# Attention with a gated MLP on one core: gating, last additions and row scaling moved from VectorE to GpSimd

## The chip, the cores and the metric

The kernel runs on one core of one Trainium2 chip. The metric is the time on the device in microseconds (us), the median of several runs. The time before is 1219.27 us, the median of 3 runs (1219.25 to 1219.4). The profile is of one execution of 1219.27 us, whose recorded span is 1217.5 us.

In the profile, PE is TensorE's matmuls, PEld its weight loads, DVE is VectorE, ACT is ScalarE, POOL is GpSimd, SP is SyncE. PSUM is the memory that matmuls write to, SBUF the on-chip memory that the other operands lie in.

## The reference

One input x (2048 rows of 512, bf16) is layer-normalised. The result feeds an attention with 32 heads against a cache of 2048 keys and values, and an MLP. The two are multiplied and added to x.

```python
xn = (x - mean) / sqrt(var + 1e-5)                 # per row of 512
q  = heads(xn @ wq)                                # 32 heads of 128
p  = softmax(q @ k_cache^T * 128 ** -0.5)          # 2048 x 2048 per head
s  = merge(p @ v_cache) @ wo                       # 2048 x 512
r  = max(xn @ w1 + b1, 0)                          # 2048 x 1792
g  = silu(r * r @ w2 + b2)                         # 2048 x 512
out = x + s * g
```

## The kernel before

The 2048 rows go in four blocks of 512 (j), each of four tiles of 128 rows (qt); jt is the tile's number, 0 to 15. Each block passes all 32 heads, each head in 8 steps of 256 keys (two tiles of 128), so that there are 1024 steps. At each step TensorE makes two score matmuls, ScalarE one exponential of 128x1024, and TensorE two matmuls with the values. All else (projections, MLP, output projection) is filled in between as single matmuls.

A small planner in the kernel's own source places every instruction on its engine's fixed list, from rough costs that it keeps of each. Three waiting lists matter here. `calm(due, fn)` puts a job on VectorE's list; `pool_quiet.append(fn)` puts one on GpSimd's list. The planner takes a job from them when it thinks that the engine is free and the job's inputs are there (`needs`).

The softmax's denominators need column sums of the exponentials pT. A pair is either reduced by VectorE alone (`den_part`), or GpSimd first adds its two halves into h_sum (`part_add`) and VectorE reduces that (`part_half`). The planner chooses by how much VectorE is behind. pT has 8 buffers, and an exponential waits until the one of 8 steps before has been read:

```python
def part_add(pi):                                   # GpSimd
    t_part[pi] = E(GP, partial(_tt, out=h_sum[:, x % NHS, :], in0=pT[:, pi % NPT, 0:QB],
                               in1=pT[:, pi % NPT, QB:2 * QB], op=ALU.add), ...)
    calm(pi + 6, partial(part_half, pi, x))          # then VectorE reduces h_sum
# ... in gen_scores:
    t_exp[pi] = E(AC, partial(_act, out=pT[:, pi % NPT, c0:c1], ..., func=ACT.Exp, ...),
                  deps=[t, t_PV[pi - NPT] ..., t_part.get(pi - NPT)])
```

The layer norm of the next block's rows (VectorE), transposed by DMA:

```python
def ln_scale(j, i):
    t_xn[jt] = E(DV, partial(_ts, out=ln_y(jt), in0=ln_x(jt),
                             scalar1=mv_t[:, i, 0:1], scalar2=rstd[:, i:i + 1],
                             op0=ALU.subtract, op1=ALU.mult), ...)
```

The gate. silu(z) = z/2 * (1 + tanh(z/2)), and the kernel keeps g_all = z * (1 + tanh(z/2)), twice the silu:

```python
# job_o2.evac: z from PSUM with the bias
tz = E(DV, partial(_tt, out=z_t[:, s, :], in0=bankF(bank), in1=b2bc[:], op=ALU.add), ...)
box[0] = E(AC, partial(_act, out=th_t[:, 0, :], in_=z_t[:, s, :], func=ACT.Tanh, scale=0.5), ...)
t_g[jt] = E(DV, partial(_stt, out=g_all[:, gs, :], in0=th_t[:, 0, :], scalar=1.0,
                        in1=z_t[:, s, :], op0=ALU.add, op1=ALU.mult), ...)
```

The output projection is summed in chunks of 8 heads into acc (float32, in SBUF). After the last but one chunk, acc is gated and x added; the last chunk is gated from PSUM and added to acc:

```python
if m == len(CH[j]) - 2:
    calm(step + 16, partial(acc_gate, j, qt))        # VectorE: acc = 0.5 * acc * g_all
    pool_quiet.append(partial(acc_add, j, qt))       # GpSimd:  acc = acc + x
if last:
    t = E(DV, partial(_stt, out=tmp_t[:, s, c0:c1], in0=place, scalar=0.5,
                      in1=g_all[:, jt % TPB, c0:c1], op0=ALU.mult, op1=ALU.mult), ...)
    eng = GP if j == NQB - 1 and qt in (0, 2) else DV
    t_fin[jt] = t_tmp[s] = E(eng, partial(_tt, out=row, in0=tmp_t[:, s, c0:c1],
                                          in1=acc[:, qt, c0:c1], op=ALU.add), ...)
    # ... and the DMA of the row to out
```

Of the kernel before, what the change touches and what calls it, by code (L numbers as in the profile page):

```python
# [5 lines left out]
ACT = mybir.ActivationFunctionType  # L6
# [53 lines left out]
def _cost(name, fn):  # L60
    f, k = fn.func, fn.keywords
    n = _elements(k["out"])
    if name == "PE":
        return n / 2.4 + 2.5, n / 2.4 + 166
    if name == "ACT":
        return n * 0.83 + 70, n * 0.83 + 172
    if name == "POOL":
        if f is _tt and n > 1:
            c = n * 2.3 + 55 if k["out"].tensor.name == "oT" else n * 2.05 + 60
            return c, c + 50  # L70
        return (500, 560) if f is _tt else (n + 100, n + 150)
    if f is _reduce_t:
        n = _elements(k["in_"])
    elif f is _reduce:
        n = _elements(k["in_"]) * 1.3 + 35
    elif f is _recip:
        n = n * 3.1
    elif f in (_bn_stats,):
        n = _elements(k["in_"])
    elif f is _ts and _in_sbuf(k["in0"]):  # L80
        n = n / 2
    return n / 0.96 + 70, n / 0.96 + 150


def _uses_port(name, fn):
    f, k = fn.func, fn.keywords
    if name == "POOL":
        return f in (_tt, _ts)
    if name == "DVE":
        if f in (_tt, _stt):  # L90
            return _in_sbuf(k["in0"]) and _in_sbuf(k["in1"])
        if f in (_ts, _copy):
            return _in_sbuf(k.get("in0", k.get("in_")))
    return False
# [206 lines left out]
def bass_recurrent_scan__mha_block_cached__dense_activation_squared_relu__prompt_kernel(  # L301
# [186 lines left out]
    def ln_y(jt):  # L488
        return out_t[:, jt - 2, :] if 2 <= jt < TPB else xn_t[:, jt % 2, :]
# [30 lines left out]
        ln_bn(j, i)  # L520
        ln_rstd(j, i)

    def ln_scale(j, i):
        jt = j * TPB + i
        assert jt < TPB or ln_prev(jt) in t_xnr
        t_xn[jt] = E(DV, partial(_ts, out=ln_y(jt), in0=ln_x(jt),
                                 scalar1=mv_t[:, i, 0:1], scalar2=rstd[:, i:i + 1],
                                 op0=ALU.subtract, op1=ALU.mult),
                     deps=[t_xr[jt], t_xnr.get(ln_prev(jt))])
# [7 lines left out]
        assert j < 2 or n_xuse[j - 2] == NFC + H  # L537

    def ln_next(j, i):
        ln_scale(j, i)  # L540
        ln_transpose(j, i)
        if i + 2 < TPB:
            ln_load(j, i + 2)
# [346 lines left out]
    def needs(fn):  # L890
        f, a = fn.func, fn.args
        if f in (den_part, part_half):
            m = b_no[a[0] // NPR]
            if m >= 2 and m - 2 not in t_sum:
                return None
            return [t_exp[a[0]]] if f is den_part else [t_part[a[0]]]
        if f in (den_sum, den_turn, den_write, den_read, den_total, den_recip, rec_write,
                 rec_read, den_scale):
            g = a[0]
            m = b_no[g]  # L900
            if f is den_sum and tiles[g] < NPR:
                return None
            first, before = {
                den_sum: (t_parts.get(g, []), t_row), den_turn: ([t_sum.get(m)], t_dw),
                den_write: ([t_row.get(m)], t_dr), den_read: ([t_dw.get(m)], t_tot),
                den_total: ([t_dr.get(m)], t_rw), den_recip: ([t_tot.get(m)], {}),
                rec_write: ([t_rec.get(m)], t_spr), rec_read: ([t_rw.get(m)], t_scale),
                den_scale: ([t_col.get(m), t_spr.get(m)], {})}[f]
            if m >= 2 and f not in (den_recip, den_scale):
                first = first + [before.get(m - 2)]  # L910
            return first
        if f is norm_recip:
            return t_oev[a[0]]
        if f is norm_scale:
            return [t_rden.get(a_no[a[0]])]
        if f is acc_gate:
            return [t_acc[a[1]], t_g.get(a[0] * TPB + a[1])]
        if f is acc_add:
            jt = a[0] * TPB + a[1]
            return [t_ug.get(jt), tok_xt.get(jt)]  # L920
        if f is ln_bn:
            return [t_xl.get(a[0] * TPB + a[1])]
        if f is ln_rstd:
            return [t_bn.get(a[0] * TPB + a[1])]
        if f is ln_next:
            return [t_xr.get(a[0] * TPB + a[1])]
        return gate_needs[fn]

    def ready_at(fn):
# [217 lines left out]
    def job_o2(j, qt):  # L1147
        jt = j * TPB + qt

        def mm(n, bank):  # L1150
            t = E(PE, partial(_mm, out=bankF(bank), lhsT=h2T[:, n, qt * P:(qt + 1) * P],
                              rhs=w2_sb[:, n, :], start=(n == 0), stop=(n == NFC - 1)),
                  deps=[tok_w2, t_bankF[bank], t_h2[j, n]], inc=(n == NFC - 1))
            if t is not None:
                assert n_w2[0] == NFC // 2
                t_o2[j, qt] = t
                t_o2j.append(jt)

        def evac(bank, step):
            s = jt % 2  # L1160
            assert jt < 1 or jt - 1 in t_g
            tz = E(DV, partial(_tt, out=z_t[:, s, :], in0=bankF(bank), in1=b2bc[:], op=ALU.add),
                   deps=[t_o2[j, qt], tok_b2, t_zrd[s], t_tmp[s]])
            box = [None]

            def gate():
                gs = jt % TPB
                t_g[jt] = t_zrd[s] = t_thr[0] = E(
                    DV, partial(_stt, out=g_all[:, gs, :], in0=th_t[:, 0, :], scalar=1.0,
                                in1=z_t[:, s, :], op0=ALU.add, op1=ALU.mult),  # L1170
                    deps=[box[0], t_fin.get(jt - TPB)])

            def tanh():
                box[0] = E(AC, partial(_act, out=th_t[:, 0, :], in_=z_t[:, s, :], func=ACT.Tanh,
                                       scale=0.5), deps=[tz, t_thr[0]])
                fn = partial(gate)
                gate_needs[fn] = [box[0]]
                calm(step + 8, fn)

            at(step + 1, tanh)  # L1180
            return tz
        return NFC, mm, evac

    t_fin = {}

    def job_wo(j, m, qt, c0=0, c1=D):
        jt = j * TPB + qt
# [15 lines left out]
        def evac(bank, step):  # L1203
# [2 lines left out]
                    t_wodone[j * H + h] = box[0]  # L1206
            place = (bankF(bank) if isinstance(bank, int) else bank[0])[:, 0:c1 - c0]
            if m == 0:
                t_acc[qt] = t = E(DV, partial(_copy, out=acc[:, qt, :], in_=place),
                                  deps=[box[0], t_fin.get(jt - TPB)])  # L1210
            elif not last:
# [1 line left out]
                                              in1=acc[:, qt, :], op=ALU.add),  # L1213
                                  deps=[box[0], t_acc[qt]])
            if m == len(CH[j]) - 2:
                calm(step + 16, partial(acc_gate, j, qt))
                pool_quiet.append(partial(acc_add, j, qt))
            if last:
                s = jt % 2
                assert all(x in t_g for x in t_o2j)  # L1220
                t = E(DV, partial(_stt, out=tmp_t[:, s, c0:c1], in0=place, scalar=0.5,
                                  in1=g_all[:, jt % TPB, c0:c1], op0=ALU.mult,
                                  op1=ALU.mult),
                      deps=[box[0], t_g[jt], t_tmp[s], t_zrd[s]])
                end = jt >= NQB * TPB - 2
                row = (x_t if end else out_t)[:, s, c0:c1]
                eng = GP if j == NQB - 1 and qt in (0, 2) else DV
                t_fin[jt] = t_tmp[s] = E(
                    eng, partial(_tt, out=row, in0=tmp_t[:, s, c0:c1],
                                 in1=acc[:, qt, c0:c1], op=ALU.add),  # L1230
                    deps=[t, t_u[jt], None if end else t_outdma[s]])
                eng, sl = (SP, sl_fin) if j == NQB - 1 else (GP, sl_out)
                dma = S.emit_dma(
                    eng, partial(_dma, out=out[0, jt * P:(jt + 1) * P, c0:c1],
                                 in_=row), sl[s], deps=[t_fin[jt]])
                if c1 == D:
                    t_outdma[s] = dma
            return t
        return nh, mm, evac

    def load_xt(jt):
        if jt < NQB * TPB:
# [3 lines left out]

    def acc_gate(j, qt):
        jt = j * TPB + qt
        t_ug[jt] = E(DV, partial(_stt, out=acc[:, qt, :], in0=acc[:, qt, :], scalar=0.5,
                                 in1=g_all[:, jt % TPB, :], op0=ALU.mult, op1=ALU.mult),  # L1250
                     deps=[t_acc[qt], t_g[jt]])


# [115 lines left out]
                                        in_=bass.AP(tensor=B_b2.tensor, offset=B_b2.offset,  # L1369
                                                    ap=[[0, P], [1, D]])), sl_b2)  # L1370

    at(62, load_b2)
    for i in range(2):
        at(140 + 8 * i, partial(load_xt, i))
    tok_w2 = None
# [14 lines left out]
    for j in range(NQB):  # L1390
        if j + 1 < NQB:
            for i in range(TPB):
# [2 lines left out]
                b = j * SPB + 8 * NPR + 4 * NPR * i  # L1395
                at(b, partial(calm, b + 32, partial(ln_bn, j + 1, i)))
                at(b, partial(calm, b + 32, partial(ln_rstd, j + 1, i)))
                at(b, partial(calm, b + 32, partial(ln_next, j + 1, i)))


    HD = D // 2
# [149 lines left out]
```

The softmax here doesn't subtract the row's maximum and nothing guards it: scores larger than these inputs give would overflow.

## Time and profile before

| | before |
|---|---|
| time, median of 3 | 1219.27 us |
| span of the profile | 1217.5 us |
| granted TensorE clock | 1.00 |
| matmul on TensorE | 1206.4 us, 6150 records |
| exponentials on ScalarE | 1036.6 us, 1025 |
| h_sum additions on GpSimd | 863.0 us, 758 |
| reductions of h_sum and of pT on VectorE | 495.2 us, 758; 215.4 us, 178 |

The busy row gives each engine's busy time and its share of the span. The chain of waits follows the last instruction back, at each step to what released it, and so names the work that set the end. A row of the groups names the operation, the tile written and the tiles read, their shapes, the count, the busy time, the mean of one in ns, and then the idle time in front of them with what ended it. In the profile's rows L239, L245, L249 and L253 are helpers through which many operations go, so the groups are told apart by their tiles. z_t is also the buffer of the last chunk's product (tmp_t is another name for it).

### The profile page before, as it was taken

The page shows a single profiled execution, that of the slowest core. Times are in us where ns is not written, and L with a number is a line of the kernel's source. Part 1 is how long each engine was busy: PE and PEld are TensorE (multiplying, and loading weights), DVE is VectorE, ACT ScalarE, POOL GpSimd, SP SyncE. Part 2 cuts the span into 40 slices and gives each one's busy share as a digit, 9 for nine tenths or more (in the row PEclk, how much of TensorE's full clock was granted, in tenths as well). Part 3 has the DMA queues.
Part 4 walks back from the last instruction along what each step waited for, and adds up shares of the span by engine and source line. Part 5 has one row for each costly group of instructions (what it writes and reads, how often), then busy time and mean ns, then how long its engine had stood idle before and what let it go on. Part 6 is the DMA issues. An engine that isn't in the chain of part 4 may idle for free.

```text
span 1217.5 us, 19712 instructions
## 1 busy us (share of the span) xinstructions
PE 1206.4 (99%) x6150; PEld 668.3 (55%) x6269; DVE 1067.2 (88%) x1865; ACT 1090.4 (90%) x1162; POOL 1064.2 (87%) x982
## 2 busy tenths in 40 slices
PE   9999999999999999999999999999999999999999
PEld 7555555555555555555555555555555555555556
DVE  4798889899999898879999999888999999889973
ACT  7898989999899898999989999999999999989995
POOL 1687999999898899999888899999998889999981
PEclk9999999999999999999999999999999999999999
DMA  9889888888778786777787777877778777677781
GB/s 209 182 202 211 193 181 168 187 170 184 179 157 178 170 161 155 164 159 153 169 167 159 171 167 166 163 163 164 163 163 167 164 164 164 158 160 164 160 156 49
DMA packets 510009, 203.47 MB, mean 167 GB/s; under 512 B 421808, under 2 KB 493744, under 8 KB 509904
## 3 DMA queue, kind: packets, MB, share of 16 engines
q1 hardware_dynamic: 507808, 198.13, 76.2%
q0 software_dynamic: 1424, 3.81, 1.1%
q8 instruction: 50, 0.82, 0.3%
q14 instruction: 55, 0.45, 0.1%
q10 hardware_dynamic: 672, 0.26, 0.1%
HBM read 128.23 MB, written 4.25 MB: 109 GB/s over the span
## 4 chain that ended last, share of the span: by engine, by line
PE 95%; DVE 3%; issue 1%; POOL 1%; ACT 0%; ACTq 0%; POOLq 0%
PE psA L226 36%; PE psO L226 32%; PE psF L226 24%; PE psO L231 3%; DVE d_part L286 1%; DVE acc L249 1%; POOL h_sum L239 0%; ACT pT L235 0%; PE psA L231 0%; DVE qt_sb L253 0%; DVE acc L239 0%; DVE d_sum L282 0%; PE psF L270 0%; POOL oT L239 0%; POOL acc L239 0%
## 5 line engine op out<-in xcount | busy, mean ns | idle before, releaser
L235 ACT ACTIVATE pT<-psA 128x1024 bf16<-128x1024 f32 x1025 | 1036.6, 1025 | 108.2 <-PE psA L226 71.2
L239 POOL TENSOR_TENSOR h_sum<-pT 128x512 f32<-128x512 bf16 x758 | 863.0, 1167 | 63.3 <-DVE d_part L286 31.0
L226 PE MATMUL psA<-qt_sb,kT 128*128 128x512 bf16 x1983 | 594.7, 379 | 3.8 <-ACT pT L235 0.7
L226 PE MATMUL psO<-pT,v_sb 128*128 128x512 bf16 x1832 | 548.1, 379 | 2.0
L286 DVE TRANSPOSE_TENSOR_REDUCE d_part<-h_sum 128x16 f32<-128x512 f32 x758 | 495.2, 678 | 18.1 <-POOL h_sum L239 17.5
L226 PEld LDWEIGHTS psA<-qt_sb,kT 128*128 128x128 bf16 x2032 | 285.5, 144 | 179.2 <-ACT pT L235 4.5
L226 PEld LDWEIGHTS psO<-pT,v_sb 128*128 128x128 bf16 x1872 | 183.2, 98 | 220.0 <-issue 0.6
L286 DVE TRANSPOSE_TENSOR_REDUCE d_part<-pT 128x32 f32<-128x1024 bf16 x178 | 215.4, 1213 | 12.1 <-ACT pT L235 11.4
L226 PE MATMUL psF<-xnT,wq_sb 128*128 128x512 bf16 (+1 forms) x510 | 166.1, 374 | 0.7 <-DVE xnT L253 0.2
L226 PE MATMUL psF<-wo_all,oT 128*128 128x512 bf16 x469 | 160.3, 379 | 0.3
L239 POOL TENSOR_TENSOR oT<-o_col,r_all 128x512 bf16<-128x512 f32 x117 | 150.2, 1284 | 11.6 <-DMA r_all<-r_scr 11.4
L253 DVE CAST qt_sb<-psF 128x512 bf16<-128x512 f32 (+1 forms) x130 | 87.1, 670 | 32.0 <-PE psF L226 28.8
L226 PE MATMUL psF<-xnT,w_sb 128*128 128x512 bf16 x218 | 75.4, 379 | 0.3
L226 PEld LDWEIGHTS psF<-xnT,wq_sb 128*128 128x128 bf16 x520 | 50.3, 98 | 45.9 <-issue 0.3
L226 PE MATMUL psF<-w_sb,h2T 128*128 128x512 bf16 x221 | 73.0, 379 | 0.1
L235 ACT ACTIVATE o_col<-psO 128x512 f32<-128x512 f32 x117 | 69.3, 592 | 0.0
L226 PEld LDWEIGHTS psF<-wo_all,oT 128*128 128x128 bf16 x480 | 46.9, 98 | 40.0
L231 PEld LDWEIGHTS psO<-v_sb,pT 128*128 128x128 bf16 x704 | 46.6, 98 | 19.0 <-ACT pT L235 0.4
L245 DVE TENSOR_SCALAR r_t<-psF,b1f 128x512 bf16<-128x512 f32 x56 | 41.5, 741 | 16.9 <-PE psF L226 15.0
L231 PE MATMUL psO<-v_sb,pT 128*128 128x129 bf16 x704 | 54.0, 220 | 0.1
L282 DVE TENSOR_REDUCE d_sum<-d_part 128x16 f32<-128x144 f32 (+3 forms) x117 | 46.2, 395 | 1.3
L249 DVE SCALAR_TENSOR_TENSOR h2T<-psF,b1f,r_t 128x512 bf16<-128x512 f32 x56 | 41.8, 746 | 1.7
(66 smaller groups left out, 377.4 us busy)
## 6 DMA issues: line engine op xcount, KB each, us to landing
v_sb<-in_A_v_cache_dram SPq DMA_DIRECT2D x508, 128.0 KB, 2.7
r_all<-r_scr SPq DMA_DIRECT2D x117, 256.0 KB, 3.9
wq_sb<-in_A_wq_dram SPq DMA_DIRECT2D x127, 128.0 KB, 3.1
wo_all<-in_A_wo_dram SPq DMA_DIRECT2D x16, 256.0 KB, 3.6
kT<-in_A_k_cache_dram SPq DMA_TRANSPOSE x254, 3.6
w_sb<-in_B_w_dram SPq DMA_DIRECT2D x14, 256.0 KB, 3.7
x_t<-in_A_x_dram POOLq DMA_DIRECT2D x16, 128.0 KB, 2.9
d_scr<-d_row SPq DMA_DIRECT2D x117, 16.0 KB, 2.5
```

The source lines that it names most:

```text
L226: return e.matmul(out, lhsT, rhs, start=start, stop=stop)
L231: return e.matmul(out, lhsT, rhs, start=start, stop=stop, skip_group_check=True)
L235: return e.activation(out, in_, func, bias=bias, scale=scale)
L239: return e.tensor_tensor(out, in0, in1, op)
L245: return e.tensor_scalar(out, in0, scalar1=scalar1, scalar2=scalar2, op0=op0, op1=op1)
L249: return e.scalar_tensor_tensor(out=out, in0=in0, scalar=scalar, in1=in1, op0=op0, op1=op1)
L253: return e.tensor_copy(out, in_)
L282: return e.tensor_reduce(out, in_, axis=AX.X, op=ALU.add)
L286: return e.tensor_reduce(out, in_, axis=AX.X, op=ALU.add, apply_transpose=True)
```

## The change

Work on SBUF tiles goes from VectorE to GpSimd: the gating of acc (all 16 tiles), the last addition of the first three blocks (12 tiles), and the row scaling of the layer norm of blocks 1 to 3 (12 tiles). To let GpSimd do the gating as a plain product, the factor 0.5 is taken into z: z_t becomes 0.5 * PSUM + 0.5 * b2 (the bias is halved once, by GpSimd), tanh is taken without its scale, and both gatings lose their factor. The last additions become jobs on GpSimd's waiting list, and the row scalings too.

```diff
-    def ln_scale(j, i):
+    def ln_scale(j, i, eng=DV):
...
-        t_xn[jt] = E(DV, partial(_ts, out=ln_y(jt), in0=ln_x(jt),
+        t_xn[jt] = E(eng, partial(_ts, out=ln_y(jt), in0=ln_x(jt),
...                                                          (ln_next)
-        ln_scale(j, i)
+        ln_scale(j, i, GP)
...                                                          (job_o2.evac)
-            tz = E(DV, partial(_tt, out=z_t[:, s, :], in0=bankF(bank), in1=b2bc[:], op=ALU.add),
+            tz = E(DV, partial(_stt, out=z_t[:, s, :], in0=bankF(bank), scalar=0.5, in1=b2bc[:],
+                               op0=ALU.mult, op1=ALU.add),
...
-                box[0] = E(AC, partial(_act, out=th_t[:, 0, :], in_=z_t[:, s, :], func=ACT.Tanh,
-                                       scale=0.5), deps=[tz, t_thr[0]])
+                box[0] = E(AC, partial(_act, out=th_t[:, 0, :], in_=z_t[:, s, :], func=ACT.Tanh),
+                           deps=[tz, t_thr[0]])
...                                                          (job_wo.evac)
-                calm(step + 16, partial(acc_gate, j, qt))
+                pool_quiet.append(partial(acc_gate, j, qt))
                 pool_quiet.append(partial(acc_add, j, qt))
...
-                t = E(DV, partial(_stt, out=tmp_t[:, s, c0:c1], in0=place, scalar=0.5,
-                                  in1=g_all[:, jt % TPB, c0:c1], op0=ALU.mult,
-                                  op1=ALU.mult),
+                t = E(DV, partial(_tt, out=tmp_t[:, s, c0:c1], in0=place,
+                                  in1=g_all[:, jt % TPB, c0:c1], op=ALU.mult),
...
-                eng = GP if j == NQB - 1 and qt in (0, 2) else DV
...
+                fn = partial(finish, jt, c0, c1, t)
+                if j == NQB - 1:
+                    finish(jt, c0, c1, t)
+                else:
+                    fin_due.add(jt)
+                    fin_needs[fn] = t
+                    pool_quiet.append(fn)
...
+    def finish(jt, c0, c1, t):
...
+        eng = DV if jt >= NQB * TPB - TPB and s else GP
+        t_fin[jt] = t_tmp[s] = E(
+            eng, partial(_tt, out=row, in0=tmp_t[:, s, c0:c1], in1=acc[:, jt % TPB, c0:c1],
+                         op=ALU.add),
...                                                          (acc_gate)
-        t_ug[jt] = E(DV, partial(_stt, out=acc[:, qt, :], in0=acc[:, qt, :], scalar=0.5,
-                                 in1=g_all[:, jt % TPB, :], op0=ALU.mult, op1=ALU.mult),
+        t_ug[jt] = E(GP, partial(_tt, out=acc[:, qt, :], in0=acc[:, qt, :],
+                                 in1=g_all[:, jt % TPB, :], op=ALU.mult),
...
-    at(62, load_b2)
+    def halve_b2():
+        nonlocal tok_b2
+        tok_b2 = E(GP, partial(_ts, out=b2bc[:], in0=b2bc[:], scalar1=0.5, scalar2=None,
+                               op0=ALU.mult), deps=[tok_b2])
+
+    at(58, load_b2)
+    at(66, halve_b2)
...
-                at(b, partial(calm, b + 32, partial(ln_next, j + 1, i)))
+                at(b, partial(pool_quiet.append, partial(ln_next, j + 1, i)))
```

More of the change, by code (lines that the diff above doesn't have):

```diff
@@ L67, in _cost @@
     if name == "POOL":
-        if f is _tt and n > 1:
+        if f in (_tt, _stt) and n > 1:
             c = n * 2.3 + 55 if k["out"].tensor.name == "oT" else n * 2.05 + 60
@@ L87, in _uses_port @@
     if name == "POOL":
-        return f in (_tt, _ts)
+        return f in (_tt, _ts, _stt)
     if name == "DVE":
@@ L926, in needs @@
             return [t_xr.get(a[0] * TPB + a[1])]
+        if f is finish:
+            jt = a[0]
+            return [fin_needs[fn], t_u.get(jt), t_outdma[jt % 2]]
         return gate_needs[fn]
@@ L1161, in evac @@
             assert jt < 1 or jt - 1 in t_g
-            tz = E(DV, partial(_tt, out=z_t[:, s, :], in0=bankF(bank), in1=b2bc[:], op=ALU.add),
+            assert jt < 2 or not {x for x in fin_due if x % 2 == s}
+            tz = E(DV, partial(_stt, out=z_t[:, s, :], in0=bankF(bank), scalar=0.5, in1=b2bc[:],
+                               op0=ALU.mult, op1=ALU.add),
                    deps=[t_o2[j, qt], tok_b2, t_zrd[s], t_tmp[s]])
@@ L1167, in gate @@
                 gs = jt % TPB
+                assert jt < TPB or jt - TPB in t_fin
                 t_g[jt] = t_zrd[s] = t_thr[0] = E(
@@ L1184, in bass_recurrent_scan__mha_block_cached__dense_activation_squared_relu__prompt_kernel @@
     t_fin = {}
+    fin_due = set()
+    fin_needs = {}
     def job_wo(j, m, qt, c0=0, c1=D):
@@ L1208, in evac @@
             if m == 0:
+                assert jt < TPB or jt - TPB in t_fin
                 t_acc[qt] = t = E(DV, partial(_copy, out=acc[:, qt, :], in_=place),
@@ L1220, in evac @@
                 assert all(x in t_g for x in t_o2j)
-                t = E(DV, partial(_stt, out=tmp_t[:, s, c0:c1], in0=place, scalar=0.5,
-                                  in1=g_all[:, jt % TPB, c0:c1], op0=ALU.mult,
-                                  op1=ALU.mult),
+                assert not {x for x in fin_due if x % 2 == s}
+                t = E(DV, partial(_tt, out=tmp_t[:, s, c0:c1], in0=place,
+                                  in1=g_all[:, jt % TPB, c0:c1], op=ALU.mult),
                       deps=[box[0], t_g[jt], t_tmp[s], t_zrd[s]])
-                end = jt >= NQB * TPB - 2
-                row = (x_t if end else out_t)[:, s, c0:c1]
-                eng = GP if j == NQB - 1 and qt in (0, 2) else DV
[L1228 to L1237, printed above, removed]
+                fn = partial(finish, jt, c0, c1, t)
[5 more added lines that the diff above has]
+                    pool_quiet.append(fn)
             return t
         return nh, mm, evac
+    def finish(jt, c0, c1, t):
+        s = jt % 2
+        end = jt >= NQB * TPB - 2
+        row = (x_t if end else out_t)[:, s, c0:c1]
+        eng = DV if jt >= NQB * TPB - TPB and s else GP
+        t_fin[jt] = t_tmp[s] = E(
+            eng, partial(_tt, out=row, in0=tmp_t[:, s, c0:c1], in1=acc[:, jt % TPB, c0:c1],
+                         op=ALU.add),
+            deps=[t, t_u[jt], None if end else t_outdma[s]])
+        eng, sl = (SP, sl_fin) if jt >= NQB * TPB - TPB else (GP, sl_out)
+        dma = S.emit_dma(
+            eng, partial(_dma, out=out[0, jt * P:(jt + 1) * P, c0:c1], in_=row), sl[s],
+            deps=[t_fin[jt]])
+        if c1 == D:
+            t_outdma[s] = dma
+        fin_due.discard(jt)
     def load_xt(jt):
```

## The prediction

> **What bounds the kernel now.** I read the page's busy row, then the busy time by windows, then who waited for whom on TensorE, then the one stretch in which the chain of waits leaves TensorE, and last the groups of instructions by shape. The busy row and the chain's engine shares:
>
> ```profile
> PE 1206.4 (99%) x6150; PEld 668.3 (55%) x6269; DVE 1067.2 (88%) x1865; ACT 1090.4 (90%) x1162; POOL 1064.2 (87%) x982
> ...
> PE 95%; DVE 3%; issue 1%; POOL 1%; ACT 0%; ACTq 0%; POOLq 0%
> ```
>
> A busy share of 99% proves little by itself, since matmul records overlap and their ends are modelled. So I look at how often a matmul starts. One quiet window, and the one with the longest stall (columns: span, then busy us and instruction count of PE, PEld, DVE, ACT, POOL, then clock, DMA share, GB/s):
>
> ```profile
> 700.00:720.00 20.00, 19.89 (x93) 10.62 (x93) 18.27 (x34) 18.19 (x20) 18.91 (x19) 1.00 0.73 162
> 600.00:620.00 20.00, 19.24 (x130) 11.61 (x131) 19.86 (x29) 17.32 (x19) 16.13 (x15) 1.00 0.82 174
> ```
>
> 93 weight loads, one for each 512-column matmul, fall in 20 us: a pitch of 0.215 us at a granted clock of 1.00. Nearly every undisturbed 20 us window between 40 and 1180 us shows 92 or 93 (windows with more hold 129-column matmuls). The groups of weight loads count 2032 + 1872 + 504 + 496 + 224 + 224 = 5352 matmuls 512 wide (scores, value products, projections without their first 16 narrow ones, output projection without its 48 narrow ones, two MLP layers). 5352 x 0.2155 = 1153 us. The 704 matmuls 129 wide run eight in 0.45 us on the chain: 40 us. So 1193 of 1217.5 us is streaming that the change does not touch. The other 24 us are the opening (about 16 us of loads, warm-up and first transposes), 2.6 us after the last matmul, and stalls. The waits of TensorE after the opening are a single entry, and the timeline shows where:
>
> ```profile
> PE psA L226 <- ACT pT L235: 0.7, 1, 0.7
> ```
>
> ```profile
> 604.34 2.25 POOL L239 TENSOR_TENSOR h_sum<-pT 128x512 f32<-128x512 bf16 x2
> 604.62 2.54 DVE L249 SCALAR_TENSOR_TENSOR acc<-acc,g_all 128x512 f32<-128x512 f32 x1
> 607.23 1.16 POOL L239 TENSOR_TENSOR acc<-acc,x_t 128x512 f32<-128x512 f32 x1 [0.64 <-DVE acc L249]
> 609.28 3.38 POOL L239 TENSOR_TENSOR h_sum<-pT 128x512 f32<-128x512 bf16 x3
> 615.09 5.01 ACT L235 ACTIVATE pT<-psA 128x1024 bf16<-128x1024 f32 x5 [1.20 <-POOL h_sum L239]
> 616.45 0.38 PE L226 MATMUL psA<-qt_sb,kT 128*128 128x512 bf16 x1 [0.70 <-ACT pT L235]
> ```
>
> Read upwards: TensorE lacks 0.70 us because the exponential came late; that waited for a pT buffer which GpSimd's addition had not released; GpSimd was late because it waited for the accumulator gating on VectorE; and the gating took 2.54 us because GpSimd's h_sum additions ran beside it. This is the only place where the work being moved reaches TensorE.
>
> **What the Trainium skill says.** "SBUF — State Buffer", Practical consequences: a VectorE instruction with two SBUF inputs contends with a GpSimd instruction that reads SBUF, and the second to start blocks. The trace agrees: the gating has both inputs in SBUF and takes 647 ns at best, 1623 at the median, 3061 at worst, while the same kind of instruction with one input in PSUM (z_t<-psF,g_all) stays at 681 to 692. "GPSIMD Engine Reference", section 3.1: about 2.6 cycles an element for two inputs, 1.03 to 1.8 for light one-input loops. 512 x 2.6 / 1.2 GHz is 1109 ns by that page; the trace has 1156 for acc<-acc,x_t, close. "Perfetto Trace Analysis", Optimizing Scalar/DVE Operations: because the two engines share a port, moving work between them may not help. That concerns engine time here, not the end, unless TensorE starves.
>
> **The change part by part.** The rows that price it (count, then busy us and mean ns):
>
> ```profile
> L249 DVE SCALAR_TENSOR_TENSOR acc<-acc,g_all 128x512 f32<-128x512 f32 x16 | 29.6, 1851 | 0.0
> L239 DVE TENSOR_TENSOR z_t<-psF,b2bc 128x512 f32<-128x512 f32 x16 | 10.9, 683 | 7.7 <-PE psF L226 7.7
> L245 DVE TENSOR_SCALAR xn_t<-x_ln,mv_t,rstd 128x512 bf16<-128x512 bf16 x14 | 9.8, 703 | 0.5 <-POOL rstd L239 0.4
> L239 DVE TENSOR_TENSOR out_t<-z_t,acc 128x512 bf16<-128x512 f32 x13 | 9.6, 735 | 0.4
> ```
>
> ```profile
> L239 POOL TENSOR_TENSOR acc<-acc,x_t 128x512 f32<-128x512 f32 x16 | 18.5, 1156 | 8.1 <-DVE acc L249 8.1
> L239 POOL TENSOR_TENSOR out_t<-z_t,acc 128x512 bf16<-128x512 f32 x1 | 1.3, 1269 | 13.1 <-DVE z_t L249 13.1
> L244 POOL TENSOR_SCALAR ident<-z_t 128x128 bf16<-128x128 f32 x1 | 0.6, 552 | 0.1
> ```
>
> VectorE loses 16 gatings, 29.6 us; 12 final additions, 12 x 0.735 = 8.8; 12 row scalings, 12 x 0.70 = 8.4. The new z_t (two operations in one, PSUM input) replaces an addition of 0.683; the pair of the MLP's first layer shows 0.746 for such a fused one, so at most 16 x 0.06 = +1.0. Dropping the factor 0.5 from the last product changes an operation's form, not its 0.69. The kernel's own planner then shifts load back: compared instruction by instruction, the changed program has 747 halved sums through GpSimd instead of 758, and 189 direct reductions on VectorE instead of 178. That adds 11 x (1.213 - 0.678) = +5.9 on VectorE and takes 11 x 1.167 = 12.8 off GpSimd. Net VectorE: -29.6 - 8.8 - 8.4 + 1.0 + 5.9 = -40 us, so about 1027 (84%).
>
> GpSimd gains 16 x 1.156 = 18.5, 12 x 1.269 = 15.2, and 12 row scalings. Their price is the weakest number: no 128x512 tensor_scalar ran on GpSimd. From 552 ns for 128 columns and 189 for one column, a straight line gives 189 + 511 x 2.86 = 1650 ns; the skill's one-input loop gives 440 to 770 ns. I take 1.0 us, 12 in all; halving the bias adds about 1. Minus 12.8 and minus the 8.1 us of waiting for gatings (which is idle time, not busy) the busy time comes to 1064 + 18.5 + 15.2 + 12 + 1 - 12.8 = 1098 us (90%). All of this lies beside the matmuls.
>
> On TensorE nothing is added or removed: the matmul order is the same for the first 84% of the program, then some projections trade places, and the count stays. ScalarE keeps its count; tanh without a scale costs the same. The end is unchanged: in the last block odd rows were already added by VectorE and even ones by GpSimd, and stay so. The sum for the span is therefore minus the 0.70 us stall, plus whatever new stall the fuller GpSimd causes.
>
> **The rivals.** First: the stall goes and nothing takes its place, 1219.27 - 0.70 = 1218.6. For it: GpSimd no longer waits for the gating at block boundaries, VectorE is relieved by some 2 us at each of the four gatings there, and eight pT buffers lie between the exponential and its reader. Second: GpSimd becomes the late one. It is already full where row scalings of the next block fall:
>
> ```profile
> 120.00:180.00 60.00, 59.69 (x273) 31.87 (x278) 50.26 (x92) 53.75 (x58) 58.97 (x55) 1.00 0.91 191
> ```
>
> 58.97 of 60 us busy, and the planner prices a row scaling at 612 ns; if it takes 1650, GpSimd falls 1 us behind each time. ScalarE already waited for GpSimd's additions ten times, 3.6 us in all, of which TensorE felt only that 0.70. A few more such waits could give stalls of 1 to 3 us: 1220 to 1222. Third: GpSimd overtakes TensorE as the bound. At 90% of the span it has 120 us to spare, and the planner cuts h_sum additions when it falls behind, so I give this 1 in 50; it would show as 1245 or more. Fourth: VectorE's relief shortens the matmul phase. It can't; TensorE starts 92 matmuls in 20 us where VectorE is busy for 15.89 of them (120 to 140 us) and 92 where it is busy for 19.93 (1120 to 1140 us).
>
> **Range and chances.** The first rival I hold at some 65%, the second at 30%. The point is 1218.8 us, a little above the first because of the second; eight times in ten between 1218.0 and 1221.5. Two per cent would be 24 us, all that is not streaming, so faster by over 2% has 0.01; slower by over 2% needs the third rival: 0.02; within 2%: 0.97.
>
> **What would show it right or wrong.** Right: 92 or 93 matmuls in the 20 us windows as before, the wait of 0.7 us of TensorE on the exponential gone, gatings of about 1.16 us on GpSimd, VectorE near 1027 us, GpSimd near 1098. The row scalings' mean on GpSimd decides my weakest term. Wrong: new waits of TensorE on pT with GpSimd's h_sum or a row scaling behind them, in the next-block stretches or at the block boundaries, or a TensorE share of the chain well below 95%.

## The result and the profile after

The changed kernel takes 1226.11 us, the median of 6 runs (1222.47 to 1226.18), against 1219.26 for the kernel before beside it. The ratio is 1.0049, with a 95% interval of 1.0036 to 1.0062. It is slower, by 6.9 us, and above the predicted range of 1218.0 to 1221.5; the prediction's 0.97 for a change within 2% holds.

The busy row and the chain's engine shares of the kernel after:

```profile
PE 1214.3 (99%) x6269; PEld 667.6 (55%) x6269; DVE 1053.8 (86%) x1825; ACT 1091.2 (89%) x1162; POOL 1102.7 (90%) x1012
...
PE 79%; DVE 9%; POOL 8%; issue 2%; ACT 1%; ACTq 0%; POOLq 0%
```

TensorE's busy share is still 99%, and would hide everything. The chain shows the difference: it passes through VectorE and GpSimd for 17% of the span, where it was 4% before, and TensorE's share fell from 95% to 79%. This is the busy time by windows, one that stayed as it was and one that did not (columns as before):

```profile
700.00:720.00 20.00, 20.00 (x94) 10.65 (x93) 18.82 (x33) 18.48 (x21) 19.83 (x20) 1.00 0.74 138
...
205.00:225.00 20.00, 18.34 (x84) 9.16 (x83) 18.09 (x33) 16.36 (x18) 18.82 (x18) 1.00 0.62 145
```

The second window in the kernel before:

```profile
205.00:225.00 20.00, 19.89 (x93) 10.65 (x94) 17.79 (x31) 18.41 (x20) 19.83 (x20) 1.00 0.78 191
```

In the quiet window the pitch is the old one, 93 weight loads in 20 us. In the other, ten of them are missing (83), and the granted clock is 1.00 in all three. So TensorE is not slower, it waits. Who it waits for, from the list of waits:

```profile
PE psF L226 <- DVE acc L253: 2.1, 2, 1.8
PE psF L226 <- DVE acc L239: 2.1, 2, 1.6
PE psA L226 <- POOL mhalf L261: 1.0, 1, 1.0
PE psF L226 <- DVE h2T L249: 0.8, 1, 0.8
PE psA L226 <- ACT pT L235: 0.8, 2, 0.5
```

The mhalf entry is the opening and was there before. The last is of the old kind, though the 0.70 us at 616 us is gone. The three others, 5.0 us in all, are new and name psF, the two PSUM banks that the projections, the MLP and the output projection share: VectorE empties them too late.

To compare kernels I add up, from the start times of the matmuls behind the first 20 us, what two starts lie apart beyond one pitch of 0.216 us, for gaps over 0.44 us. That sum of stalls is 0.9 us before and 7.3 us after, a difference of 6.4 of the 6.9 us by which the spans differ (1224.4 and 1217.5). (0.2 of the 0.9 us, at 303 us, is no stall: the record of one matmul is missing there, whose weight load is present. The same 0.2 us is in the sums of a6 and a5 below.) The stalls lie at 212, 222, 523, 548, 562, 739, 750, 786 and 828 us. None is at the block boundaries where accumulators are gated (276 to 306, 579 to 610 and 880 to 919 us). The row scalings of the layer norm run at 106, 128, 167, 213, 396, 438, 469, 514, 706, 742, 778 and 817 us, so five of the nine stalls, 5.2 of the 7.3 us, lie within 11 us behind a row scaling's start. That is a hint, no more. The groups by shape (count, busy us, mean ns, then idle time in front and its releaser), first of the kernel after:

```profile
L245 POOL TENSOR_SCALAR xn_t<-x_ln,mv_t,rstd 128x512 bf16<-128x512 bf16 x12 | 24.9, 2079 | 0.0
L239 POOL TENSOR_TENSOR acc<-acc,g_all 128x512 f32<-128x512 f32 x16 | 18.5, 1158 | 1.4 <-DVE g_all L249 0.8 <-DVE acc L239 0.6
```

```profile
L286 DVE TRANSPOSE_TENSOR_REDUCE d_part<-h_sum 128x16 f32<-128x512 f32 x747 | 499.1, 686 | 67.6 <-POOL h_sum L239 65.5
...
L249 DVE SCALAR_TENSOR_TENSOR g_all<-th_t,z_t 128x512 bf16<-128x512 bf16 x16 | 32.1, 2008 | 0.0
```

The last two in the kernel before:

```profile
L286 DVE TRANSPOSE_TENSOR_REDUCE d_part<-h_sum 128x16 f32<-128x512 f32 x758 | 495.2, 678 | 18.1 <-POOL h_sum L239 17.5
...
L249 DVE SCALAR_TENSOR_TENSOR g_all<-th_t,z_t 128x512 bf16<-128x512 bf16 x16 | 16.8, 1047 | 0.0
```

A row scaling takes 2.079 us on GpSimd, where it took 0.703 on VectorE. VectorE's idle time in front of its reductions of h_sum, ended by GpSimd, rose to 65.5 us; it had been 17.5. And the gate product, untouched by the change, went from 1047 to 2008 ns, with 5.10 us at worst (at 199 us). A row scaling and the late h_sum behind it, in the timeline of the kernel after:

```profile
212.54 2.08 POOL L245 TENSOR_SCALAR xn_t<-x_ln,mv_t,rstd 128x512 bf16<-128x512 bf16 x1
...
214.59 3.38 POOL L239 TENSOR_TENSOR h_sum<-pT 128x512 f32<-128x512 bf16 x3
...
215.78 0.71 DVE L286 TRANSPOSE_TENSOR_REDUCE d_part<-h_sum 128x16 f32<-128x512 f32 x1 [0.78 <-POOL h_sum L239]
...
219.16 5.61 POOL L239 TENSOR_TENSOR h_sum<-pT 128x512 f32<-128x512 bf16 x5
...
221.47 0.71 DVE L286 TRANSPOSE_TENSOR_REDUCE d_part<-h_sum 128x16 f32<-128x512 f32 x1 [0.41 <-POOL h_sum L239]
222.11 1.20 DVE L286 TRANSPOSE_TENSOR_REDUCE d_part<-pT 128x32 f32<-128x1024 bf16 x1
223.24 0.65 DVE L239 TENSOR_TENSOR acc<-psF,acc 128x512 f32<-128x512 f32 x1
223.94 0.39 PE L226 MATMUL psF<-wo_all,oT 128*128 128x512 bf16 x1 [1.58 <-DVE acc L239]
```

GpSimd works without a gap and its h_sum come late; VectorE's list is fixed, so it stands before each late h_sum although a finished PSUM bank waits further down. That bank's last matmul ended at 218.9 us, it is emptied at 223.9, and TensorE has lost 1.58 us.

### The profile page after: what moved, and what is told of

Same layout as the page of the kernel before. It is cut to its first block, busy times and chain, and to the rows that moved or that the text cites. A ratio compares the mean times of both kernels' runs of the same rounds, so it can differ in the third digit from the quotient of the medians.

```text
span 1224.4 us, 19795 instructions
## 1 busy us (share of the span) xinstructions
PE 1214.3 (99%) x6269; PEld 667.6 (55%) x6269; DVE 1053.8 (86%) x1825; ACT 1091.2 (89%) x1162; POOL 1102.7 (90%) x1012
## 4 chain that ended last, share of the span: by engine, by line
PE 79%; DVE 9%; POOL 8%; issue 2%; ACT 1%; ACTq 0%; POOLq 0%
PE psA L226 29%; PE psO L226 26%; PE psF L226 20%; POOL h_sum L239 7%; DVE d_part L286 5%; PE psO L231 3%; DVE g_all L249 2%; DVE qt_sb L253 1%; ACT pT L235 1%; POOL oT L239 1%; POOL xn_t L245 0%; DVE d_sum L282 0%; PE psA L231 0%; POOL rstd L239 0%; DVE acc L239 0%
## 5 line engine op out<-in xcount | busy, mean ns | idle before, releaser
L239 POOL TENSOR_TENSOR h_sum<-pT 128x512 f32<-128x512 bf16 x747 | 843.7, 1161 | 51.0 <-ACT pT L235 25.4
L226 PE MATMUL psA<-qt_sb,kT 128*128 128x512 bf16 x2032 | 605.5, 380 | 0.8 <-ACT pT L235 0.8
L286 DVE TRANSPOSE_TENSOR_REDUCE d_part<-h_sum 128x16 f32<-128x512 f32 x747 | 499.1, 686 | 67.6 <-POOL h_sum L239 65.5
L226 PE MATMUL psO<-pT,v_sb 128*128 128x512 bf16 x1872 | 556.8, 379 | 0.0
L286 DVE TRANSPOSE_TENSOR_REDUCE d_part<-pT 128x32 f32<-128x1024 bf16 x189 | 227.7, 1209 | 5.3 <-ACT pT L235 4.7
L226 PE MATMUL psF<-xnT,wq_sb 128*128 128x512 bf16 (+1 forms) x520 | 169.1, 374 | 0.2 <-DVE xnT L253 0.2
L226 PE MATMUL psF<-wo_all,oT 128*128 128x512 bf16 x480 | 163.5, 379 | 4.3 <-DVE acc L253 2.1
L245 DVE TENSOR_SCALAR r_t<-psF,b1f 128x512 bf16<-128x512 f32 x56 | 40.9, 730 | 19.5 <-PE psF L226 18.6
L282 DVE TENSOR_REDUCE d_sum<-d_part 128x16 f32<-128x144 f32 (+4 forms) x117 | 47.2, 403 | 2.3
```

The costliest lines, as they stand in the source:

```text
L226: return e.matmul(out, lhsT, rhs, start=start, stop=stop)
L239: return e.tensor_tensor(out, in0, in1, op)
L245: return e.tensor_scalar(out, in0, scalar1=scalar1, scalar2=scalar2, op0=op0, op1=op1)
L282: return e.tensor_reduce(out, in_, axis=AX.X, op=ALU.add)
L286: return e.tensor_reduce(out, in_, axis=AX.X, op=ALU.add, apply_transpose=True)
```

## The experiments

Two theories stood at the start. Theory 1: the row scaling alone makes the loss, since it takes 2.08 us where the kernel's planner reckons with 0.61, so that GpSimd is late against its plan. Theory 2: GpSimd is too full, whatever it is filled with. The kernel before was run beside each group of experiments and moved by up to 1.4 us between groups (medians 1219.2, 1220.6, 1219.2 and 1219.3), so each ratio is within its own group.

### One part back, or one part alone

a1, the row scaling back on VectorE:

```diff
-        ln_scale(j, i, GP)
+        ln_scale(j, i)
-                at(b, partial(pool_quiet.append, partial(ln_next, j + 1, i)))
+                at(b, partial(calm, b + 32, partial(ln_next, j + 1, i)))
```

> The changed kernel with the layer norm's row scaling put back on VectorE; gating and last additions stay on GpSimd. Theory 1 (the row scaling, 2.08 us on GpSimd where the planner reckons with 0.61, makes GpSimd late, and all the loss comes from there): TensorE's stalls after 20 us fall from 7.3 us to under 1 and the time is 1218.3 to 1219.5. Theory 2 (GpSimd is too full whatever it is filled with: 34 us of gating and last additions are as bad as 25 us of row scaling): a good half of the loss stays, 1222 to 1226, and VectorE's gate product still has cases of over 3 us.

a2, the same edit the other way round, in the kernel before: nothing but the row scaling moves.

> The kernel before with nothing but the row scaling moved to GpSimd. Theory 1: most of the loss comes with this part alone, 1222 to 1228, with stalls of TensorE within some 15 us behind a row scaling. Theory 2: 12 x 2.08 us is less than half of what was added to GpSimd, so 1220 to 1222 at most.

a4, the changed kernel with the gating back on VectorE:

```diff
-                pool_quiet.append(partial(acc_gate, j, qt))
+                calm(step + 16, partial(acc_gate, j, qt))
-        t_ug[jt] = E(GP, partial(_tt, out=acc[:, qt, :], ...
+        t_ug[jt] = E(DV, partial(_tt, out=acc[:, qt, :], ...
```

> The changed kernel with the gating of acc put back on VectorE (as a plain product). The gatings lie at the block boundaries, the stalls do not, so theory 1 expects the loss to stay, 1223 to 1227, perhaps with the 0.7 us stall at a block boundary back. Theory 2 expects a third to a half of the loss to go, 1221 to 1223.5.

b3, only the gating on GpSimd: a1's edit, and the last additions back too:

```diff
-                if j == NQB - 1:
+                if True:
                     finish(jt, c0, c1, t)
...
-        eng = DV if jt >= NQB * TPB - TPB and s else GP
+        eng = GP if jt >= NQB * TPB - TPB and not s else DV
```

> The changed kernel with the row scaling and the last additions back on VectorE; only the gating of acc (and the halved bias) is on GpSimd. Floor from the kernel before without its stall of 0.7 us: 1218.5. Theory 1: 1218.4 to 1219.3, as good as the kernel with only the row scaling put back, or better by its remaining stall of 0.5. If the last additions on GpSimd matter: better by more than that, or worse by over 1 us if VectorE needed the relief.

a5, the last additions back, the row scaling and the gating on GpSimd (b3's edit without a1's):

> The changed kernel with the last additions back on VectorE; row scaling and gating on GpSimd. Theory 1: the row scaling is still there, so most of the loss stays, 1222 to 1227; the last additions alone explain at most 1 us either way.

a6, only the last additions on GpSimd (a1's and a4's edits together):

> Only the last additions on GpSimd (row scaling and gating on VectorE, with the halved bias). It completes the eight combinations of the three parts but for the two that are the kernels before and after. Theory 1: within 1 us of before, 1218.5 to 1220, with the stall at the block boundary still possible since the gating is on VectorE.

Measured, in the order of what is on GpSimd (stalls are the sum explained above, from each one's profile):

| on GpSimd | kernel | median us | ratio to before, 95% interval | stalls us |
|---|---|---|---|---|
| nothing | before | 1219.26 | | 0.9 |
| last additions | a6 | 1219.43 | 1.0000 (0.9992 to 1.0008) | 1.0 |
| gating | b3 | 1218.83 | 0.9989 (0.9980 to 0.9997) | 0.0 |
| gating, last additions | a1 | 1218.99 | 0.9999 (0.9991 to 1.0007) | 0.5 |
| row scaling | a2 | 1231.02 | 1.0092 (1.0078 to 1.0106) | 11.3 |
| row scaling, last additions | a4 | 1227.65 | 1.0072 (1.0059 to 1.0084) | 7.1 |
| row scaling, gating | a5 | 1234.59 | 1.0124 (1.0111 to 1.0137) | 13.0 |
| all three | after | 1226.11 | 1.0049 (1.0036 to 1.0062) | 7.3 |

Before and a2 have the whole bias, the others the halved one. All four kernels without the row scaling on GpSimd lie within 0.11% of before, all four with it are 0.5 to 1.2% slower. Theory 2 falls with one comparison: in a1 GpSimd is busy for 1092.8 us and in a2 for 1080.5, and a2 is the one that loses 12 us. The expectation of a2 was missed upwards (1222 to 1228 expected), that of a4 by 0.65 us (1223 to 1227), and that of a5 clearly (1222 to 1227): there the last additions' going back costs 8.5 us instead of at most 1. The parts do not add up. Each kernel is planned anew, and presumably it differs from list to list where a late GpSimd meets a full VectorE; this was not followed. The way to TensorE differs too: in a2 the largest entry of its waits is for exponentials, 5.3 us, and 4.1 us are for psF. What is stable is the sign of the row scaling.

The gating alone on GpSimd is a small gain, 0.1%. The chain of waits of b3, shares by engine:

```profile
PE 99%; ACT 0%; DVE 0%; ACTq 0%; issue 0%; POOL 0%; POOLq 0%
```

TensorE does not stall at all behind the opening, and the span is 1216.6 us against 1217.5.

### The planner told the price

a3, the changed kernel, with the cost that its planner keeps for a tensor_scalar on GpSimd set to what was measured:

```diff
     if name == "POOL":
+        if f is _ts and n > 1:
+            c = n * 3.85 + 60
+            return c, c + 50
```

> The changed kernel, the same work on the same engines, but the planner is told 2.03 us for a 512-column tensor_scalar on GpSimd instead of 0.61; it then sends 740 instead of 747 halved sums through GpSimd. If theory 1 holds in the form that the planning error is the cause (GpSimd late against its plan), nearly all of the loss goes: 1218.3 to 1220. If it is the load itself (a 2 us instruction blocks what stands behind it, or GpSimd is too full, theory 2), it stays at 1222 to 1226.

Measured: 1221.85 us, 1.0026 (1.0018 to 1.0034), stalls 3.3 us. Between the two expectations: better than the changed kernel, and not as good as without the row scaling. What is left in its profile is one stall of 0.6 and one of 2.7 us, the latter at 810 us behind a gate product of 4.45 us at 799. Between the two it is not GpSimd that is awaited: GpSimd stands idle itself, 1.31 us up to 804.4 and 1.16 us up to 809.3, waiting for VectorE. So with the right price about half of the loss goes, and most of what is left comes about in another way. But the lists changed with the price, and this run alone can't say more.

### An idle load in the same places

Four kernels have the row scaling on VectorE as in a1, and give GpSimd something useless at the places of the row scalings, priced at 0.61 us in all: tensor_scalars or memsets of 128 columns into a tile that nobody reads.

```diff
+    def ln_hold(j, i):
+        for c in range(3):          # b1; 2 in b6.  b2: 7 memsets; b5: 10 memsets
+            t_hold[0] = E(GP, partial(_ts, out=ident[:], in0=w1_sb[:, 0, c * P:(c + 1) * P],
+                                      scalar1=mhalf[:], scalar2=mhalf[:], ...), ...)
...
+                at(b, partial(pool_quiet.append, partial(ln_hold, j + 1, i)))
```

b1: 

> The kernel with the row scaling back on VectorE (gating and last additions on GpSimd), and at the places where GpSimd had a row scaling it now does three tensor_scalar of 128 columns into a tile that nobody reads, about 2.1 us together, priced by the planner at 0.61 as the row scaling was. No result comes later than before. If GpSimd's time, unplanned, is what costs: 1223 to 1229, stalls behind these places. If it was the scaled rows' being late (or VectorE's list without the scaling): 1218.5 to 1219.6.

b2: 

> The same, with seven memsets of 128 columns (about 2 us together, priced at 0.61) in the place of the three tensor_scalar: GpSimd is held as long but reads nothing from SBUF. If lateness alone costs: as the idle scaling, 1223 to 1229. If VectorE suffers from GpSimd's reading of SBUF during the row scaling itself: clearly less, 1219 to 1221.

b5: 

> As the kernel with idle memsets, but ten of them in each place: 2.6 us, as long as the three idle tensor_scalar, still priced at 0.61. If the length of the unplanned occupation decides, it loses as the idle scaling does: 1226 to 1230. If GpSimd's reading of SBUF matters too (it holds up VectorE's two-input gate product): clearly less, 1220 to 1224.

b6: 

> As the kernel with idle scaling, but two tensor_scalar of 128 columns instead of three: 1.7 us, as long as the seven memsets, priced at 0.61. If length decides: 1219.5 to 1222, as the seven memsets. If reading matters: well above them, 1223 to 1227.

| | in each place | median us | ratio to before, 95% interval |
|---|---|---|---|
| b1 | 3 tensor_scalar, 2.6 us | 1229.03 | 1.0075 (1.0061 to 1.0089) |
| b6 | 2 tensor_scalar, 1.7 us | 1221.07 | 1.0014 (1.0007 to 1.0021) |
| b5 | 10 memsets, 2.6 us | 1221.18 | 1.0020 (1.0012 to 1.0028) |
| b2 | 7 memsets, 1.8 us | 1221.28 | 1.0006 (0.9998 to 1.0014) |

b1 suggests that the scaled rows need not be late: useless work that nobody waits for costs as much as the changed kernel's row scaling or more. b5 came out as expected if reading mattered: it and b1, equally long, differ by 0.5%. b6 came out as expected if length alone decided: it agrees with b2. But the lists of these four on VectorE and GpSimd differ from one another, because the planner treats a memset and a tensor_scalar differently, and prices them singly. The comparison was spoilt.

### The same lists

So I made three kernels whose lists are the same in every other instruction on all engines: the planner charges 0.61 us at each place, and what really stands there is nothing (c0), ten memsets (c1) or three tensor_scalars (c2).

```diff
+    def ln_hold(j, i):
+        GP.t = max(GP.t, S.ready([t_xr[j * TPB + i]])) + 612
+        t0, last = GP.t, GP.last
+        ...                          # c0: nothing; c1: ten memsets; c2: three tensor_scalar
+        GP.t, GP.last = t0, last
```

c0: 

> Row scaling on VectorE, gating and last additions on GpSimd; the planner charges GpSimd 0.61 us at the places of the row scalings, but nothing is placed there. It is the base for the next two, whose lists are the same in every other instruction on all engines. 1218.5 to 1219.6 under either theory, since GpSimd is then ahead of its plan.

c1: 

> The same lists with ten memsets of 128 columns (2.6 us, GpSimd reads nothing) at each place. If lateness alone costs: as much as the next kernel, 1222 to 1229. If GpSimd's reading is needed for the loss: 1218.5 to 1221.

c2: 

> The same lists with three tensor_scalar of 128 columns (2.6 us, GpSimd reads SBUF). If lateness alone costs: the same as the memsets within 1 us. If reading matters: 3 us or more above them.

The fourth keeps the changed kernel's own lists, and GpSimd's row scaling computes only 128 of its 512 columns; three quarters of the normalised rows of blocks 1 to 3 are left out:

```diff
+        if k["out"].tensor.name == "xn_t":
+            return 612, 662
...
+        w = P if eng is GP else D
-        t_xn[jt] = E(eng, partial(_ts, out=ln_y(jt), in0=ln_x(jt),
+        t_xn[jt] = E(eng, partial(_ts, out=ln_y(jt)[:, 0:w], in0=ln_x(jt)[:, 0:w],
```

c3: 

> The changed kernel with all its lists as they are, but GpSimd's row scaling computes only the first 128 of 512 columns (the rest of the normalised rows is left out), about 0.8 us instead of 2.08, so nearly what the plan says. If the 1.3 us too many, twelve times, are the cause of the loss: 1218.3 to 1219.6, with stalls of under 1 us in all. If the row scaling's place in GpSimd's list, or the lists as such, are the cause: 1222 to 1226 as before.

| | in each place | median us | ratio to before, 95% interval | stalls us |
|---|---|---|---|---|
| c0 | nothing | 1218.53 | 0.9992 (0.9984 to 1.0001) | 0.0 |
| c1 | 10 memsets, 2.6 us | 1225.23 | 1.0050 (1.0037 to 1.0063) | 5.1 |
| c2 | 3 tensor_scalar, 2.6 us | 1225.96 | 1.0058 (1.0045 to 1.0072) | 5.2 |
| c3 | the row scaling, 128 columns, 0.80 us | 1218.28 | 0.9988 (0.9980 to 0.9996) | 0.0 |

c1 and c2 are 6.7 and 7.4 us above c0 and agree within 0.8 us. So GpSimd's time beyond the plan is enough, and neither a late row nor the added instructions' reading of SBUF is needed. c3 settles the cause: with every list as in the changed kernel, taking 1.28 us off each of twelve row scalings takes all of the loss away, to a little below the kernel before. The timeline of c3 at the place shown above for the kernel after:

```profile
210.09 0.79 POOL L247 TENSOR_SCALAR xn_t<-x_ln,mv_t,rstd 128x128 bf16<-128x128 bf16 x1
210.85 3.38 POOL L241 TENSOR_TENSOR h_sum<-pT 128x512 f32<-128x512 bf16 x3
...
215.43 6.73 POOL L241 TENSOR_TENSOR h_sum<-pT 128x512 f32<-128x512 bf16 x6
```

```profile
217.73 0.71 DVE L288 TRANSPOSE_TENSOR_REDUCE d_part<-h_sum 128x16 f32<-128x512 f32 x1 [0.40 <-POOL h_sum L241]
218.36 1.20 DVE L288 TRANSPOSE_TENSOR_REDUCE d_part<-pT 128x32 f32<-128x1024 bf16 x1
219.49 0.65 DVE L241 TENSOR_TENSOR acc<-psF,acc 128x512 f32<-128x512 f32 x1
```

The same three VectorE instructions in the same order, 3.75 us earlier (219.49 against 223.24): 2.45 of it GpSimd's being earlier already at the row scaling (210.09 against 212.54), the rest the row scaling itself. The bank is empty before TensorE wants it.

As the lists are the same, the lateness can be followed back. This is the row scaling before that one, first in the kernel after, then in c3:

```profile
166.46 2.08 POOL L245 TENSOR_SCALAR xn_t<-x_ln,mv_t,rstd 128x512 bf16<-128x512 bf16 x1
```

```profile
165.49 0.80 POOL L247 TENSOR_SCALAR xn_t<-x_ln,mv_t,rstd 128x128 bf16<-128x128 bf16 x1
```

GpSimd is 0.97 us later than in c3 in front of it, and 2.24 us behind it (its next instruction starts at 168.50 and at 166.26). The 2.24 us are still there, as 2.45, at the row scaling of 212.54, and that one makes 3.74 of them. In between GpSimd does stand idle for 2.0 us, from 204.0 to 206.0, but it waits for VectorE there, and VectorE's gate product ends only when GpSimd's run before it is over, 0.55 us behind it in both kernels (204.56 here, 202.08 in c3). So VectorE has taken over the lateness, and hands it back.

The gate product's long turns are not the cause by themselves: c3 has two of 4.03 and 4.45 us and no stall. They are in part an effect: with the same lists, the 16 gate products take 22.3 us in c3 and 32.1 in the kernel after, 16.7 in c0 and 29.4 in c1. What they add to the stalls in their turn was not separated.

### What a tensor_scalar costs on GpSimd

b4 is a1 with 21 instructions on GpSimd behind all its work, where VectorE has little or nothing left to do (w1_sb lends bf16 data, o_col float32, mhalf the scalars):

```diff
+    for _ in range(3):               # and so on, seven forms, each three times
+        tf.append(E(GP, partial(_ts, out=r_t[:, 0, 0:512], in0=w1_sb[:, 0, 0:512],
+                  scalar1=mhalf[:], scalar2=mhalf[:], op0=ALU.subtract, op1=ALU.mult), deps=tf))
```

> The kernel with the row scaling back on VectorE, and behind all its work 21 instructions on GpSimd, alone: tensor_scalar of 512 bf16 columns with two scalars from SBUF, with two constants, with one constant and one operation; 256 columns; float32 in; float32 out; and a tensor_tensor of bf16. Straight line through 190 ns (one column) and 2079 (512): 3.7 ns a column. If the cost is in the scalars from SBUF, the constants' form takes half or less, about 1.0 us; if it is one pass per operation, one operation takes about 1.1 us (the halving of the bias, one operation with a constant, took 1504 in the loaded kernel, which speaks against half); 256 columns 1.13 us by the line.

Its timeline on GpSimd (start, length of three with their gaps; L245 has two operations, L244 one; with mhalf the scalars come from SBUF, without it they are constants):

```profile
1212.92 6.70 POOL L245 TENSOR_SCALAR r_t<-w_sb,mhalf 128x512 bf16<-128x512 bf16 x3
1219.71 5.94 POOL L245 TENSOR_SCALAR r_t<-w_sb 128x512 bf16<-128x512 bf16 x3
1225.73 4.65 POOL L244 TENSOR_SCALAR r_t<-w_sb 128x512 bf16<-128x512 bf16 x3
1230.48 3.87 POOL L245 TENSOR_SCALAR r_t<-w_sb,mhalf 128x256 bf16<-128x256 bf16 x3
1234.45 6.42 POOL L245 TENSOR_SCALAR r_t<-o_col,mhalf 128x512 bf16<-128x512 f32 x3
1240.96 6.41 POOL L245 TENSOR_SCALAR h_sum<-w_sb,mhalf 128x512 f32<-128x512 bf16 x3
1247.46 3.60 POOL L239 TENSOR_TENSOR r_t<-w_sb 128x512 bf16<-128x512 bf16 x3
```

Each length holds two gaps of about 0.1 us. The single instructions take 2.07 us with scalars from SBUF (the first of all 2.36), 1.92 with constants, 1.49 with one operation, 1.22 for 256 columns, 2.07 with float32 on either side, and 1.15 for the tensor_tensor. The 2.07 us are the 2.079 of the row scaling in the kernel after. So the cost is the instruction itself, not the data type or a neighbour, and the scalars' place makes 0.15 us of it: a tensor_scalar with one operation takes 0.34 us longer than a product of two tensors, and a second operation adds another 0.43. Neither of the two guesses in the expectation holds.

## Why the prediction was wrong

**The bound.** Right. The pitch of 0.215 us and the granted clock stayed, the end stayed, and 6.4 of the 6.9 us are TensorE's stalls.

**The stall of 0.70 us at a block boundary.** Right, and it carries over: gatings take 1.158 us on GpSimd (1.156 predicted), and in b3, where only they move, no stall is left.

**VectorE.** 1027 us predicted, 1053.8 measured. The removed work went as reckoned. The gate product, taken as unchanged, takes 15.3 us more (32.1 against 16.8), and the reductions of h_sum 3.9 more (499.1 against 495.2) instead of 7.5 less.

**GpSimd.** 1098 us predicted, 1102.7 measured, and the closeness is luck of the sum: the row scalings take 24.9 us instead of 12, and the h_sum additions fall by 19.3 us (863.0 to 843.7) instead of 12.8.

**The step that failed: the price of the row scaling, and what hung on it.** The prediction called it its weakest number, had 1650 ns from a straight line, and took 1.0 us, leaning to the skill's figures. In the Trainium skill, "GPSIMD Engine Reference", section 3.1, has 1.03 to 1.8 cycles an element for light loops, by estimate 440 to 770 ns for 512, without naming tensor_scalar, and section 4.1 calls one-input work roughly line-rate; here it is 2079 ns, and the measurement decides. The straight line was nearer. Its 128 columns were an instruction with one operation, for which 1650 ns is fair (1494 in b4, 1504 for the halving of the bias); the row scaling has two. With 1.0 us GpSimd would overrun its plan by 0.4 us each time; it overruns by 1.47, twelve times, 17.6 us.

**The rivals.** The mechanism was the second rival, "GpSimd becomes the late one", in the stretches where the next block's rows are scaled. Two things about it were wrong. The path to TensorE: I put the first rival at 65% on the strength of eight pT buffers, but in the kernel after only 0.8 us of TensorE's waits come through pT and 5.0 through psF, which has two banks and is emptied by VectorE, whose fixed list stands behind late h_sum. (Where the row scaling moves alone, in a2, the path that I had named counts too: 5.3 us through pT.) And the size, 1 to 3 us of stalls, was taken from ScalarE's waits; it was 7.3. Rivals three and four are out: GpSimd at 90% is not the bound (a1 has the same 90% and no loss), and VectorE's relief shortens nothing (18 us less in a1, at the time of before).

**Moving work between the two engines.** In the Trainium skill, "Perfetto Trace Analysis", Optimizing Scalar/DVE Operations, says that it may not help. The runs show both: the gating helps by the stall it removes, the row scaling harms. The contention that "SBUF — State Buffer", Practical consequences, describes shows in the gate product, from 0.63 us at best to 5.10. The row scaling's own part in it is not needed for the loss, for c1 (memsets, which read nothing) loses about as much as c2. But the h_sum additions read SBUF in all these kernels, and what they add by holding up the gate product stays open; the stall of 2.7 us in a3 suggests that it is not nothing.

**Left open.** Why a5 loses 15 us and the changed kernel 7, which differ in the last additions alone, was not followed through their lists. Nor was it shown why half of the loss stays in a3, where GpSimd's plan is right.

## What to carry to other kernels

When work moves to another engine in a kernel whose order is fixed beforehand, measure the very instruction there first: what counts is not the receiver's busy share but how far the instruction overruns what the plan allows. An overrun of 1.5 us, twelve times, on an engine that was never the bound cost 7 us, because in-order neighbours pass it on until a scarce buffer, here mostly the two PSUM banks, runs out. The overrun does not give the size of the loss: ten memsets, 2.0 us over their plan, cost 0.5% in c1 and 0.2% in b5, whose lists differ. And to tell a cause from a reshuffled plan, compare kernels whose lists are otherwise the same.

## What the runs showed of the hardware

On GpSimd a tensor_scalar of 128x512 with two operations (1.92 to 2.08 us) is slower than a tensor_tensor of the same size (1.15 us), although it reads one tensor less. On VectorE, the gate product with two inputs in SBUF was held for 5.10 us at worst while GpSimd ran three h_sum additions and a scaling of oT without a gap beside it; at best it takes 0.63 us.
